# A transformer block on one core: a 1152x1152 matrix-vector section moved from TensorE to VectorE, with its weights loaded transposed and the loads around it reordered

## The chip, the core and the metric

The kernel runs on one core of a Trainium2 chip. The metric is device time in microseconds (us) of one execution. Most executions of one kernel agree within 0.3%. A profile is one execution recorded by the hardware profiler; its "span" is mostly some 1.8 us shorter than the device time of the same run, because the start and the end of the program are not in it. Engines: PE is TensorE (PEld its weight loads), DVE is VectorE, ACT is ScalarE, POOL is GpSimd, and SP is SyncE, which here does nothing but issue transfers.

## The reference

One block of a diffusion transformer: two batches (B = 2) of N = 256 tokens, width D = 1152 (9 times 128), two heads, MLP width 4608, bf16.

```python
mod = (_silu(c) @ w_mod).reshape(B, 6, 1, D)
shift_a, scale_a, gate_a, shift_m, scale_m, gate_m = [mod[:, i] for i in range(6)]
h = _layernorm(x, axis=-1) * (1 + scale_a) + shift_a
q, k, v = ...                       # h @ wqkv
attn = _softmax(jnp.einsum('bqhd,bkhd->bhqk', q, k) * Dh ** (-0.5), axis=-1)
a = jnp.einsum('bhqk,bkhd->bqhd', attn, v).reshape(B, N, D) @ wo
x = x + gate_a * a
h2 = _layernorm(x, axis=-1) * (1 + scale_m) + shift_m
m = _gelu(h2 @ w_fc1) @ w_fc2
return x + gate_m * m
```

Each of the six modulation sections is a product of two rows (`s = silu(c)`, one per batch) with a 1152x1152 slice of `w_mod`: 2.65 MB of weights for very little arithmetic. This case is about one of them, `scale_m`, which is not needed before the MLP.

## The kernel before

TensorE does the work in this order: K, Q, scores, V, attention times V of the first batch, output projection of the first batch, attention times V of the second batch, the two MLP sections `shift_m` and `scale_m`, output projection of the second batch, f1 (first MLP matrix), f2 (second). All weights come through one queue that SyncE feeds in program order. The parts that matter:

```python
# a section on TensorE: s is the stationary operand (32 columns wide), the weights are streamed: 36 matmuls
def vec_section(stat, w, name): ...
shift_m = vec_section(sT, w_shift_m, "shift_m")
scale_m = vec_section(sT, w_scale_m, "scale_m")
nc.vector.tensor_scalar_add(scale_m[:, :, 0:B], scale_m[:, :, 0:B], 1.0)
# ... used by the modulation of the second layer norm, in front of f1
```

```python
# a section on VectorE, as this kernel already does gate_m, late in the MLP where the engine is idle
def dot_section(wT, s_all, spill, dst):
    for j in range(KD):                       # KD = 9
        for b in range(B):
            nc.vector.scalar_tensor_tensor(
                spill, wT[:, j, :], 1.0, s_all[:, b, :], op0=ALU.mult, op1=ALU.mult,
                accum_out=dst[:, b * KD + j:b * KD + j + 1])
```

For this the weights must lie with the output column on the partition, so they are loaded by transposing transfers (`dma_start_transpose`), and the row `s` is broadcast to all partitions. The order of the loads on the queue, as the program gives it:

```python
w_q, w_v, w_gate_a, w_o, w_shift_m          # issued before the attention part
attn_transpose(0); attn_transpose(1)        # softmax results, transposed by a transfer SBUF to SBUF
w_scale_m, w_f1_0                           # behind the attention transposes
ln2_transpose(0) ... (3)                    # layer norm results, transposed the same way, into hT
w_f1_1 ... w_f1_3, s_all, w_gate_mT         # the last one by transposing transfers
```

Copies of the results of Q, V and attention times V out of PSUM alternate between VectorE and ScalarE (`evac`), and the first `MSPLIT = 8` row blocks of f1 are done one batch at a time, so that they can start before the second batch's modulation is finished.

## Time and profile before

The median is 245.28 us in three runs (245.0 to 245.95).

The timeline of TensorE in the stage that the change touches (start, length, line, what it did; a bracket would say how long the engine sat idle before it, and for what):

```profile
74.03 1.91 PE L530 MATMUL pa<-attnT_all,big 128*128 128x256 bf16 x16
75.87 0.63 PE L546 MATMUL pa<-attnT_all,big 128*64 128x256 bf16 x8
76.43 9.16 PE L612 MATMUL pacc<-w_o,big 128*128 128x384 bf16 x54
85.43 1.91 PE L530 MATMUL pa<-attnT_all,big 128*128 128x256 bf16 x16
...
88.38 1.28 PE L365 MATMUL pn<-w_scale_m,sT 128*32 128x288 bf16 x36
89.59 8.97 PE L612 MATMUL pacc<-w_o,big 128*128 128x384 bf16 x63
98.40 9.80 PE L707 MATMUL pacc<-hT,w_f 128*128 128x256 bf16 x82
```

No bracket: TensorE waits for nothing. The line of `w_scale_m` is what the change takes away; with the 36 matmuls of `w_shift_m`, left out here, it takes 2.32 us in the chain. And the timeline of SyncE, which shows when a transfer was handed to the queue and how long SyncE was held by it:

```profile
60.17 8.40 SPq L490 DMA_TRANSPOSE attnT_all<-soft  x2
...
127.86 15.03 SPq L685 DMA_TRANSPOSE w_gate_mT<-in_w_mod_dram  x3
```

The first transpose of attention is issued at 60.17; the records of its semaphore show it complete at 70.14, 3.9 us before TensorE needs it. The other line is for transposing loads of weights: three of 0.885 MB, of which the second and third took SyncE 4.02 and 4.13 us. A plain load of the same size takes 2.4 to 2.7 us.

### The profile page before, as it was taken

What the parts mean: (1) busy time and instruction counts of PE and PEld (TensorE: products, weight loads), DVE (VectorE), ACT (ScalarE), POOL (GpSimd) and SP (SyncE); (2) the same over time, 40 slices, a digit from 0 to 9 for tenths busy, and PEclk for the clock granted to TensorE, in tenths of its full rate; (3) what the DMA queues carried; (4) which work ended last, traced back from release to release, by engine and by line L of the source; (5) the groups of instructions that cost most, each with busy time, mean ns of one, the idle gap of its engine ahead of it and who ended that gap; (6) DMA issues with size and microseconds to landing.
All of it is one profiled execution on the core that took longest, in us unless ns stands there. A gap on an engine that the chain in (4) does not pass through costs nothing.

```text
span 243.1 us, 3903 instructions
## 1 busy us (share of the span) xinstructions
PE 237.1 (98%) x1652; PEld 139.4 (57%) x1652; DVE 83.7 (34%) x194; ACT 66.7 (27%) x130; POOL 31.3 (13%) x47
## 2 busy tenths in 40 slices
PE   8899999999999999999999999999999999999994
PEld 2585444465656676978444444444665666656674
DVE  3752462115635676720000019999002000000001
ACT  7632250133614075773322222333000000000000
POOL 1000013000310615200000000000314211111111
PEclk9999999999999999999999999999999999999999
DMA  6999999999999992299999999999891000000000
GB/s 231 328 334 362 370 327 313 363 362 336 374 235 347 342 193 49 49 236 330 326 327 273 246 206 337 327 326 280 240 282 49 16 19 16 16 20 27 22 16 19
DMA packets 70813, 53.89 MB, mean 222 GB/s; under 512 B 18939, under 2 KB 65419, under 8 KB 70795
## 3 DMA queue, kind: packets, MB, share of 16 engines
q1 hardware_dynamic: 70064, 52.43, 74.1%
q0 software_dynamic: 704, 1.20, 1.8%
q8 instruction: 13, 0.21, 0.4%
q14 instruction: 5, 0.04, 0.1%
q10 hardware_dynamic: 27, 0.00, 0.0%
HBM read 48.08 MB, written 1.19 MB: 203 GB/s over the span
## 4 chain that ended last, share of the span: by engine, by line
PE 93%; DMA 3%; DVE 1%; SPq 0%; ACT 0%; issue 0%; DVEq 0%
PE pacc L707 29%; PE pacc L767 29%; PE pacc L612 7%; PE pacc L503 7%; PE pacc L438 7%; PE pk L253 4%; DMA w_scale_a<-in_w_mod_dram 3%; PE pk L282 2%; PE pn L365 1%; PE pa L530 1%; PE ps_s L458 1%; PE pm L221 1%; DVE stats L163 1%; PE pt L231 1%; PE pg L398 0%; SPq L85 0%
## 5 line engine op out<-in xcount | busy, mean ns | idle before, releaser
L707 PE MATMUL pacc<-hT,w_f 128*128 128x512 bf16 (+1 forms) x396 | 71.0, 340 | 0.0
L767 PE MATMUL pacc<-w_f,gT 128*128 128x384 bf16 (+2 forms) x468 | 70.5, 314 | 0.0
L767 PEld LDWEIGHTS <-gT 128*128 128x128 bf16 x468 | 44.3, 98 | 26.3
L707 PEld LDWEIGHTS <-w_f 128*128 128x128 bf16 x396 | 38.7, 98 | 31.9 <-issue 0.7
L429 DVE SCALAR_TENSOR_TENSOR late<-w_gate_mT,late 128x1152 bf16<-128x1152 bf16 x18 | 24.4, 1357 | 38.0 <-DMA w_gate_mT<-in_w_mod_dram 37.4
L773 DVE TENSOR_TENSOR tmp<-pacc,gate 128x384 f32<-128x384 f32 (+2 forms) x13 | 6.8, 526 | 62.6 <-PE pacc L767 50.3
L744 ACT ACTIVATE gT<-pacc 128x512 bf16<-128x512 f32 x28 | 16.7, 597 | 37.7 <-PE pacc L707 37.7
L612 PE MATMUL pacc<-w_o,big 128*128 128x384 bf16 (+2 forms) x117 | 18.1, 314 | 0.0
L503 PE MATMUL pacc<-w_v,hT 128*128 128x384 bf16 x108 | 17.9, 326 | 0.0
L775 POOL TENSOR_TENSOR o_sb<-tmp,x 128x384 bf16<-128x384 f32 (+1 forms) x12 | 11.6, 972 | 47.6 <-DVE tmp L773 47.6
L438 PE MATMUL pacc<-hT,w_q 128*128 128x512 bf16 x81 | 17.7, 379 | 0.0
L612 PEld LDWEIGHTS <-big 128*128 128x128 bf16 x117 | 10.9, 98 | 7.1 <-DVE big L270 0.6
L503 PEld LDWEIGHTS <-hT 128*128 128x128 bf16 x108 | 10.4, 98 | 7.2 <-issue 0.5
L253 PE MATMUL pk<-big,w_k 128*128 128x256 bf16 (+2 forms) x90 | 13.4, 294 | 0.4 <-ACT big L240 0.4
L438 PEld LDWEIGHTS <-w_q 128*128 128x128 bf16 x81 | 7.8, 98 | 9.8 <-DMA w_q<-in_wqkv_dram 0.5
L618 POOL TENSOR_TENSOR x<-tmp,x_sb 128x384 f32<-128x384 f32 (+1 forms) x11 | 9.8, 888 | 17.4 <-DVE tmp L617 10.7
L420 POOL DMA_DIRECT2D gates_dram<-grow x4 | 2.0, 512 | 71.4 <-DVE grow L730 71.4
L253 PEld LDWEIGHTS <-w_k 128*128 128x128 bf16 x90 | 7.5, 97 | 3.4 <-DMA w_k<-in_wqkv_dram 0.3
L146 PE MATMUL pwarm<-zeros 128*128 128x512 bf16 x23 | 7.7, 483 | 1.2 <-DVE eps_t L92 1.2
L617 DVE TENSOR_TENSOR tmp<-pacc,gate 128x384 f32<-128x384 f32 (+2 forms) x13 | 6.7, 525 | 5.4 <-PE pacc L612 5.3
L595 ACT ACTIVATE hT<-hT,shift_m,scale_m 128x256 bf16<-128x256 bf16 x12 | 6.2, 588 | 3.8 <-DVE stats L624 3.3
L240 ACT ACTIVATE big<-pt,scale_a 128x256 bf16<-128x256 bf16 (+1 forms) x12 | 4.6, 434 | 9.3 <-PE pt L231 7.6
(96 smaller groups left out, 146.8 us busy)
## 6 DMA issues: line engine op xcount, KB each, us to landing
w_f<-in_w_fc_dram SPq DMA_DIRECT2D x14, 864.0 KB, 10.9
w_f<-in_w_fc_dram SPq DMA_DIRECT2D x2, 2592.0 KB, 11.8
w_f<-in_w_fc_dram SPq DMA_DIRECT2D x2, 1728.0 KB, 14.9
w_shift_a<-in_w_mod_dram SPq DMA_DIRECT2D x3, 864.0 KB, 11.3
w_q<-in_wqkv_dram SPq DMA_DIRECT2D x3, 864.0 KB, 12.0
w_v<-in_wqkv_dram SPq DMA_DIRECT2D x3, 864.0 KB, 10.5
w_gate_a<-in_w_mod_dram SPq DMA_DIRECT2D x3, 864.0 KB, 9.9
w_o<-in_wo_dram SPq DMA_DIRECT2D x3, 864.0 KB, 13.8
```

Source lines behind the costliest of these rows:

```text
L146: nc.tensor.matmul(dst[:], zeros[:, 0:P], zeros[:], start=True, stop=True)
L253: nc.tensor.matmul(pk[m][:, c0:c1], w_k[:, k, m * P:(m + 1) * P], hT0[:, k, c0:c1], start=(k == 0 and c0 == 0), stop=(k == KD - 1), skip_g ...
L429: nc.vector.scalar_tensor_tensor(spill, wT[:, j, :], 1.0, s_all[:, b, :], op0=ALU.mult, op1=ALU.mult, accum_out=dst[:, b * KD + j:b * KD + ...
L438: nc.tensor.matmul(pacc[:], w_q[:, k, m * P:(m + 1) * P], hT[:, k, :], start=(k == 0), stop=(k == KD - 1),)
L503: nc.tensor.matmul(pacc[:], hT[:, k, t * P:(t + 1) * P], w_v[:, k, pnl * PW:(pnl + 1) * PW], start=(k == 0), stop=(k == KD - 1),)
L612: nc.tensor.matmul(pacc[:], aT[:, k, t * P:(t + 1) * P], w_o[:, k, c0:c1], start=(k == 0), stop=(k == KD - 1),)
L618: (nc.vector if (t, i) in ((1, 2), (3, 3)) else nc.gpsimd).tensor_tensor(x1[:, t, c0:c1], tmp[:], x_sb[:, t, c0:c1], op=ALU.add)
L707: nc.tensor.matmul(dst, w_f1[m // KD][:, k, ml * P:(ml + 1) * P], hT[:, k, c0:c1], start=(k == 0), stop=(k == KD - 1),)
L744: nc.scalar.activation(gT[:, m, :], pacc[:], ACT.Gelu_apprx_tanh)
L767: nc.tensor.matmul(pacc[:], gT[:, kk, t * P:(t + 1) * P], w_f2[j][:, r, c0 - n * PW:c0 - n * PW + cw], start=(kk == 0), stop=(kk == KF - 1),)
L773: nc.vector.tensor_tensor(tmp[:], pacc[:], gate_m[:, b, c0:c0 + cw], op=ALU.mult)
L775: (nc.vector if last else nc.gpsimd).tensor_tensor(o_sb[:], tmp[:], x1[:, t, c0:c0 + cw], op=ALU.add)
```

## The change

The intent: take the 36 matmuls of `scale_m` (half of 2.32 us) off the engine that bounds the kernel, by giving them to VectorE, which is 34% busy, as 18 multiply-accumulate passes of 1.36 us. For that the section has to come transposed, and earlier, in slices between the loads of Q and V, and VectorE is relieved of the copies of Q and V. The core of the diff:

```diff
+    s_b = [work.tile([P, D], BF16, name="s_b", tag="xn", bufs=4) for _ in range(B)]
+    for b in range(B):
+        nc.sync.dma_start(s_b[b][:], s_dram[b:b + 1, :].partition_broadcast(P))
+    load_transposed(w_scale_mT, S_SCALE_M, 0)
+    load_panel(w_q, wqkv_v, 0, 2)
+    load_panel(w_v, wqkv_v, 2 * D, 0)
+    load_transposed(w_scale_mT, S_SCALE_M, CPP)
+    load_section("w_gate_a", S_GATE_A, w_gate_a)
+    load_panel(w_v, wqkv_v, 2 * D, 1)
+    load_panel(w_v, wqkv_v, 2 * D, 2)
+    load_transposed(w_scale_mT, S_SCALE_M, 2 * CPP)
+    w_o = load_panels("w_o", wo_v, 0)
...
+    scale_m_passes(0, KD)                      # nine passes ahead of Q's copies and softmax
     for m in range(KD):
...
-        evac(qT[:, m, :], pacc[:], attn_scale)
+        nc.scalar.mul(qT[:, m, :], pacc[:], attn_scale)
...
-        evac(v_sb[:, t, pnl * PW:(pnl + 1) * PW], pacc[:])
+        nc.scalar.copy(v_sb[:, t, pnl * PW:(pnl + 1) * PW], pacc[:])
...
-        if i == 1:
+        if i == 2:
+            scale_m_passes(KD, B * KD)         # nine passes behind the last softmax piece
+        if i == TPB + 1:
             gate_a = gate_natural(0, w_gate_a)
...
-    w_scale_m = load_section("w_scale_m", S_SCALE_M)
+    w_shift_m = load_section("w_shift_m", S_SHIFT_M)   # now behind the attention transposes
...
-    scale_m = vec_section(sT, w_scale_m, "scale_m")
-    nc.vector.tensor_scalar_add(scale_m[:, :, 0:B], scale_m[:, :, 0:B], 1.0)
...
-    MSPLIT = 8
+    MSPLIT = KD
```

(The two comments are added here. Left out: the rows `s` are written to DRAM earlier, so that they can be broadcast.) The product of `gate_a` also uses a wider stationary operand and one copy in place of four.

More of the change, by code (lines that the diff above doesn't have):

```diff
@@ L121, with load_panel, load_transposed @@
     w_shift_a = load_section("w_shift_a", S_SHIFT_A)
-    w_q = load_panels("w_q", wqkv_v, 0)
+    w_q = wide_tile("w_q")
+    w_scale_mT = wide_tile("w_scale_mT")
+    w_v = wide_tile("w_v")
     w_gate_a = wide_tile("w_gate_a")
-    w_v = load_panels("w_v", wqkv_v, 2 * D)
-    load_section("w_gate_a", S_GATE_A, w_gate_a)
-    w_o = load_panels("w_o", wo_v, 0)
-    w_shift_m = load_section("w_shift_m", S_SHIFT_M)
+    def load_panel(w, view, col0, n):
+        nc.sync.dma_start(w[:, :, n * PW:(n + 1) * PW], view[:, :, col0 + n * PW:col0 + (n + 1) * PW])
+    def load_transposed(w, s, j):
+        c0 = s * D + j * P
+        nc.sync.dma_start_transpose(w[:, j:j + CPP, :], w_mod[:, c0:c0 + PW])
+    load_panel(w_q, wqkv_v, 0, 0)
+    load_panel(w_q, wqkv_v, 0, 1)
     big1 = act.tile([P, 4 * KD, T], BF16, name="big1", tag="big")
@@ L285, in k_panel, with store_by_quadrant @@
             )
+    s_dram = tc.dram_tile([B, D], BF16, name="s_dram")
+    def store_by_quadrant(dst, src, rows):
+        for a in range(4):
+            nc.gpsimd.dma_start(dst[a], src[32 * a:32 * a + rows])
+    s_rows = work.tile([P, KD, SW], BF16, name="s_rows", tag="s_rows", bufs=1)
     CUT = 4 * P
@@ L299 @@
     norm1(0, 0, CUT, "d")
+    nc.vector.transpose(s_rows[:].rearrange("p k c -> p (k c)"), sT[:].rearrange("p k c -> p (k c)"))
+    store_by_quadrant(s_dram[:].rearrange("b (k a r) -> a b k r", a=4, r=32), s_rows, B)
     add0()
@@ L389, with scale_m_passes @@
     k_evac(8)
+    s_b = [work.tile([P, D], BF16, name="s_b", tag="xn", bufs=4) for _ in range(B)]
+    s_spill = work.tile([P, D], BF16, name="s_spill", tag="xn", bufs=4)
+    for b in range(B):
[9 more added lines that the diff above has]
+    w_o = load_panels("w_o", wo_v, 0)
+    scale_m = act.tile([P, KD, B], FP32, name="scale_m")
+    def scale_m_passes(p0, p1):
+        dot_passes(
+            w_scale_mT, [t[:] for t in s_b], s_spill[:], lambda j, b: scale_m[:, j, b:b + 1], range(p0, p1),
+        )
     gates_dram = tc.dram_tile([2, B, D], BF16, name="gates_dram")
@@ L398, in gate_natural @@
                 nc.tensor.matmul(
-                    pn[32 * i:32 * i + B, :], sT[:, k, 0:B], wg[:, k, i * CTW:(i + 1) * CTW],
+                    pn[32 * i:32 * i + SW, :], sT[:, k, :], wg[:, k, i * CTW:(i + 1) * CTW],
                     start=(k == 0), stop=(k == KD - 1), tile_position=(0, 32 * i),
@@ L402, in gate_natural @@
         nat = work.tile([P, CTW], BF16, name="nat", tag="nat", bufs=1)
+        nc.scalar.copy(nat[:], pn[:])
         for i in range(4):
             rows = slice(32 * i, 32 * i + B)
-            if i % 2 == 0:
-                nc.vector.tensor_copy(nat[rows, :], pn[rows, :])
-            else:
-                nc.scalar.copy(nat[rows, :], pn[rows, :])
             nc.gpsimd.dma_start(gates_dram[g, :, i * CTW:(i + 1) * CTW], nat[rows, :])
@@ L413, in gate_natural, with dot_passes @@
         return gate
-    s_dram = tc.dram_tile([B, D], BF16, name="s_dram")
-    def store_by_quadrant(dst, src, rows):
-        for a in range(4):
-            nc.gpsimd.dma_start(dst[a], src[32 * a:32 * a + rows])
-    s_rows = work.tile([P, KD, SW], BF16, name="s_rows", tag="s_rows", bufs=1)
-    nc.vector.transpose(s_rows[:].rearrange("p k c -> p (k c)"), sT[:].rearrange("p k c -> p (k c)"))
-    store_by_quadrant(s_dram[:].rearrange("b (k a r) -> a b k r", a=4, r=32), s_rows, B)
-    def dot_section(wT, s_all, spill, dst):
-        for j in range(KD):
-            for b in range(B):
-                nc.vector.scalar_tensor_tensor(
-                    spill, wT[:, j, :], 1.0, s_all[:, b, :], op0=ALU.mult, op1=ALU.mult,
-                    accum_out=dst[:, b * KD + j:b * KD + j + 1],
-                )
-    gate_a = None
+    def dot_passes(wT, s_b, spill, dst, passes):
+        for i in passes:
+            j, b = divmod(i, B)
+            nc.vector.scalar_tensor_tensor(
+                spill, wT[:, j, :], 1.0, s_b[b], op0=ALU.mult, op1=ALU.mult, accum_out=dst(j, b),
+            )
+    scale_m_passes(0, KD)
     for m in range(KD):
@@ L551, in pv_shared @@
         evac(aT[:, HC, :], pa[:].rearrange("p b q n -> p (b q n)"))
+    nc.vector.tensor_scalar_add(scale_m[:], scale_m[:], 1.0)
     pv_chunks(0, 0)
@@ L587, in ln2_transpose @@
         nc.sync.dma_start_transpose(hT[:, :, t * P:(t + 1) * P], xn2[t][:])
-    shift_m = scale_m = None
     def ln2_modulate(b, ks=range(KD)):
@@ L710, in f1_mm @@
         )
-    MSPLIT = 8
+    MSPLIT = KD
     for b in range(B):
         for m0 in range(0, MSPLIT, 2):
-            pacc = acc_tile([P, 2, N], "pacc")
-            for m in (m0, m0 + 1):
+            ms = range(m0, min(m0 + 2, MSPLIT))
+            pacc = acc_tile([P, len(ms), N], "pacc")
+            for m in ms:
                 for k in range(KD):
                     f1_mm(pacc[:, m - m0, :], m, k, b * N, (b + 1) * N)
-            if b == 0 and m0 == MSPLIT - 2:
+            if b == 0 and ms[-1] == MSPLIT - 1:
                 ln2_modulate(1)
-            nc.scalar.activation(gT[:, m0:m0 + 2, b * N:(b + 1) * N], pacc[:], ACT.Gelu_apprx_tanh)
+            nc.scalar.activation(gT[:, ms[0]:ms[-1] + 1, b * N:(b + 1) * N], pacc[:], ACT.Gelu_apprx_tanh)
     gcol = small.tile([P, SW], FP32, name="gcol", tag="gcol", bufs=1)
@@ L745 @@
         if m == 14:
-            dot_section(w_gate_mT, s_all, late[:, B, :], gcol)
+            dot_passes(
+                w_gate_mT, [s_all[:, b, :] for b in range(B)], late[:, B, :],
+                lambda j, b: gcol[:, b * KD + j:b * KD + j + 1], range(B * KD),
+            )
             gate_m = gate_m_finish()
```

## The prediction

> **What bounds the kernel now.** TensorE. The busy table gives PE 237.1 of 243.1 us (98%), and the chain of waits is 93% PE; from 33.5 us to the end it never leaves PE for more than 0.1 us. DMA is the hidden second limit: the slices show it full from 6 to about 85 us (300 to 390 GB/s), so loads there are only moved, not hidden.
>
> **What the change removes.** 36 matmuls on w_scale_m: the pair of section products takes 2.32 us in the chain (87.3 to 89.7), so half, 1.16 us, all critical. MSPLIT 9 instead of 8 keeps PE on the first batch's half about 1 us longer (8 steps take 7.86 us); the trace shows second-half matmuls spaced out at 106.4 to 107.7 while modulation (0.34 us a piece) catches up. Worth about 0.6 us. Together: -1.75 us.
>
> **What it adds.** 18 VectorE passes at 1.357 us plus 0.08 us of accumulator read, 1.40 us apart in the trace (the gate_m passes): 25.2 us. 12.6 us of them come before softmax, 12.6 us after it. Off the engine's total this is free (DVE is 34% busy); by position it is not:
> - First nine: the transposed chunk 0 lands at about 42 us, chunk 1 at about 52 us, so they end at about 56, where softmax's first maximum wants DVE at 55.05: 0.5 to 1 us late.
> - Last nine: program order puts them after the last softmax piece (ends 66.6 before; about 65 to 66 now without V copies on DVE). They end at 78 to 79. The attention-times-V copies that stay on DVE were taken from 74.7 before. The output projection then waits until about 78.7 for its third chunk, where PE arrives at about 76.8: about 2 us lost.
>
> **DMA.** w_scale_m's 2.65 MB move ahead of the attention transposes (shift_m moves behind them), as transposed loads. The gate_m ones are issued 4.0 to 4.1 us apart for 0.885 MB, that is about 217 GB/s, against 2.4 to 2.7 us for plain panels: some 4.5 us extra, plus 1.8 us for the two broadcast rows. The Trainium skill, "DMA: Bandwidth & Descriptors", section "Latency and other measured facts", gives 261 GB/s for transposed DMA; this trace is slower, and I use the trace. The same page ("Queues, rings and completion order") says a ring is consumed in order, so the attention transposes queue behind w_o. They landed at about 70.2 us before and were needed at 74; now I estimate 76.5 to 77.7, so PE waits about 3 us. This overlaps the DVE delay above, not adds to it. q panel 2 (needed 45.2, lands about 45) and v panel 1 (needed 62.4, lands about 62) are just in time; gate_a's broadcast lands at about 80, near its need.
>
> ScalarE takes all Q and V copies (0.60 and 0.48 us each); it fits.
>
> **Sum.** +3.3 us lost around 74 to 80 us, -1.75 us gained later: about 246.7 us. An 80% range: 244.1 to 249.3. Chances: faster by over 2% 0.01, within 2% 0.93, slower 0.06.
>
> **What would show it.** Right: the chain of waits leaves PE near 74 to 79 us, for the DMA of attnT_all or for DVE passes; waits of the attention-times-V or output-projection matmuls grow from under 0.6 to 2 to 4 us; span from there to the end shorter by about 1.7 us; the f1 matmuls run without gaps at the batch change. Wrong: attnT_all lands before 74 us, or DVE passes end before 75.
>
> **What would make it wrong.** Transposed loads of 384-column strips running near plain speed (then about 245.2, the DVE delay alone); a much later q panel 2 or chunk 1 delaying softmax (248 or more); softmax finishing earlier, so that even DVE is in time (about 243.6).

## More of the kernel before

The head of the page of the profile: the busy line, then from the 40 slices the rows of TensorE, of its granted clock (9 is 90% or more of full speed) and of the bytes that the transfers moved, then the chain of work that ended last.

```profile
span 243.1 us, 3903 instructions
...
PE 237.1 (98%) x1652; PEld 139.4 (57%) x1652; DVE 83.7 (34%) x194; ACT 66.7 (27%) x130; POOL 31.3 (13%) x47
...
PE   8899999999999999999999999999999999999994
...
PEclk9999999999999999999999999999999999999999
...
GB/s 231 328 334 362 370 327 313 363 362 336 374 235 347 342 193 49 49 236 330 326 327 273 246 206 337 327 326 280 240 282 49 16 19 16 16 20 27 22 16 19
...
PE 93%; DMA 3%; DVE 1%; SPq 0%; ACT 0%; issue 0%; DVEq 0%
```

TensorE is busy 98% of the span, at full clock throughout, and the chain is TensorE work nearly everywhere. The row of GB/s shows the second thing to know: up to slice 14 (about 85 us) the queue of transfers is full. A load that is added there does not fill a hole, it pushes everything behind it.

## The result, and the profile after

The changed kernel takes 251.59 us (median of six runs, 250.38 to 251.99), against 245.45 for the kernel before in the same rounds (six runs, 244.97 to 246.12). The ratio is 1.0242, with a 95% interval of 1.0213 to 1.0271: slower by over 2%. Ratios are the mean time of one kernel's fast runs over that of the other's of the same rounds, so they are not quite the ratio of the medians quoted. The outputs are right.

The same parts of the page as above:

```profile
span 249.3 us, 3878 instructions
...
PE 238.2 (96%) x1615; PEld 140.5 (56%) x1625; DVE 100.5 (40%) x216; ACT 71.8 (29%) x141; POOL 31.4 (13%) x47
...
PE   7899999999993999999999999999999999999994
...
PEclk9999999999997799999999999999999999999999
...
GB/s 236 325 323 362 365 262 266 263 336 349 214 323 348 385 326 126 25 100 320 329 326 332 214 222 276 328 329 327 199 317 102 32 16 18 16 17 18 16 31 16
...
PE 56%; ACT 2%; DMA 1%; issue 1%; DVE 0%; ACTq 0%; DVEq 0%
```

There is one hole, in the slice that holds 75 to 81 us, and beside it a dent in the clock. TensorE has 36 matmuls fewer and yet 1.1 us more busy time. The chain of work that ended last now leads from f1 back through the layer norm (ACT, a transfer) and is traced no further back than 96.14 us, so its shares cover only the time from there; it does not pass through the hole, which therefore has to be read from the waits and the timeline. Its timeline, beside the one above:

```profile
79.02 3.60 PE L556 MATMUL pa<-attnT_all,big 128*128 128x256 bf16 x16 [4.60 <-DMA attnT_all<-soft]
82.55 1.06 PE L572 MATMUL pa<-attnT_all,big 128*64 128x256 bf16 x8
83.54 9.31 PE L638 MATMUL pacc<-w_o,big 128*128 128x384 bf16 x54
92.69 1.91 PE L556 MATMUL pa<-attnT_all,big 128*128 128x256 bf16 x16
...
95.75 8.97 PE L638 MATMUL pacc<-w_o,big 128*128 128x384 bf16 x63
104.55 1.10 PE L731 MATMUL pacc<-hT,w_f 128*128 128x256 bf16 x8
105.88 2.34 PE L731 MATMUL pacc<-hT,w_f 128*128 128x256 bf16 x20 [0.22 <-ACT hT L621]
```

Subtract the start times of the same stages, and the whole 6.2 us of difference in span falls out, with its sign:

| what | us | from |
|---|---|---|
| everything up to the end of V | +0.39 | 79.02 - 4.60 against 74.03 (0.2 of it is there when Q starts) |
| wait for the transposed attention | +4.60 | the bracket |
| attention times V and the shared heads take 4.52 us, not 2.40 | +2.12 | 79.02 to 83.54, against 74.03 to 76.43 |
| first output projection | +0.15 | 83.54 to 92.69, against 76.43 to 85.43 |
| second batch's attention, then one section, not two | -1.10 | 92.69 to 95.75, against 85.43 to 89.59 |
| second output projection | -0.01 | 95.75 to 104.55, against 89.59 to 98.40 |
| f1 to the end | +0.05 | 144.75 against 144.7; the eight matmuls at 104.55 take 1.33 us for 0.87 us of work, so 0.46 us of gap is inside |

The second large term is not a wait. The windows view (busy time of each engine in a stretch, then the granted clock, the share of the transfer engines and GB/s) of the changed kernel:

```profile
76.00:78.00 2.00, 0.00 (x0) 0.00 (x0) 1.93 (x5) 0.00 (x0) 0.00 (x0) 0.87 1.21 368
78.00:80.00 2.00, 0.98 (x5) 0.73 (x6) 0.05 (x1) 0.00 (x0) 0.00 (x0) 0.50 1.10 316
...
84.00:86.00 2.00, 2.00 (x13) 1.13 (x11) 0.43 (x1) 1.58 (x2) 0.00 (x0) 0.92 1.04 387
```

The granted clock falls to one half at 77.49, some 3.1 us after TensorE fell idle, and is back at 84.31, so the matmuls that follow the wait run at half speed (one every 213 ns in place of one every 109). This is what the Trainium skill says on "TensorE: Matmul & The Clock Gate", Part 1, "What's actually happening": the clock drops to one half after an idle window of about 3.4 us and comes back after a busy one, and the window is free-running. This trace agrees, and so do the others: each spell of half clock inside a kernel is one or two times 3.41 us long (6.83 here, 3.41 in e1, e3, e8 and e12). Of the six runs of the changed kernel two have the mean clock of one such window (0.993), four that of two (0.984 to 0.986).

Why the transposed attention was late, in the timeline of SyncE:

```profile
31.92 6.77 SPq L132 DMA_TRANSPOSE w_scale_mT<-in_w_mod_dram  x1
...
40.00 8.84 SPq L132 DMA_TRANSPOSE w_scale_mT<-in_w_mod_dram  x1
...
55.91 9.41 SPq L132 DMA_TRANSPOSE w_scale_mT<-in_w_mod_dram  x1
65.42 4.04 SPq L118 DMA_DIRECT2D w_o<-in_wo_dram  x3
69.55 7.20 SPq L514 DMA_TRANSPOSE attnT_all<-soft  x2
```

Before, SyncE issued the first attention transpose at 60.17; now at 69.55, because it stands behind a transposing load that holds SyncE for 9.41 us and behind `w_o`. The semaphore records have it complete at 78.97 (70.14 before), and TensorE starts at 79.02.

VectorE, finally. This group line gives count, busy time and mean of the new passes, then the idle time before them with its releaser:

```profile
L454 DVE SCALAR_TENSOR_TENSOR s_spill<-w_scale_mT,s_b 128x1152 bf16<-128x1152 bf16 x18 | 24.4, 1358 | 7.8 <-DMA w_scale_mT<-in_w_mod_dram 7.3
```

The first nine end at 55.2, and softmax's first maximum is at 55.25, against 55.05 before: no delay. The last nine end at 77.84. VectorE was done before the transposed attention came.

So the first comparison leaves two theories for the 6.1 us:

- Theory A: the transposing loads, standing in the queue ahead of the attention transposes, cost much more queue time than assumed; the wait of 4.6 us and the halved clock that follows are consequences.
- Theory B (rival): VectorE is the real limit at that point. Its last nine passes end at 77.84, the copies that follow could not have started earlier, so even with timely transposes most of the loss would remain.

There are two smaller questions: what the halved clock alone costs, and where the expected gain of 1.75 us (1.16 for the matmuls, 0.6 for MSPLIT) has gone, as f1 to the end is no shorter.

### The profile page after: what moved, and what is told of

Same layout as the page of the kernel before. It is cut to its first block, busy times and chain, and to the rows that moved or that the text cites. A ratio compares the mean times of both kernels' runs of the same rounds, so it can differ in the third digit from the quotient of the medians.

```text
span 249.3 us, 3878 instructions
## 1 busy us (share of the span) xinstructions
PE 238.2 (96%) x1615; PEld 140.5 (56%) x1625; DVE 100.5 (40%) x216; ACT 71.8 (29%) x141; POOL 31.4 (13%) x47
## 4 chain that ended last, share of the span: by engine, by line
PE 56%; ACT 2%; DMA 1%; issue 1%; DVE 0%; ACTq 0%; DVEq 0%
PE pacc L795 28%; PE pacc L731 28%; ACT hT L621 2%; DMA hT<-xn 1%; ACT xn L604 0%; ACT rstd L595 0%; DVE tmp L801 0%; DVE o_sb L803 0%; ACTq L621 0%; DVEq L801 0%
## 5 line engine op out<-in xcount | busy, mean ns | idle before, releaser
L731 PEld LDWEIGHTS <-w_f 128*128 128x128 bf16 x405 | 39.6, 98 | 31.2 <-issue 0.8
L454 DVE SCALAR_TENSOR_TENSOR s_spill<-w_scale_mT,s_b 128x1152 bf16<-128x1152 bf16 x18 | 24.4, 1358 | 7.8 <-DMA w_scale_mT<-in_w_mod_dram 7.3
L769 ACT ACTIVATE gT<-pacc 128x512 bf16<-128x512 f32 x27 | 16.1, 597 | 36.5 <-PE pacc L731 36.5
L556 PE MATMUL pa<-attnT_all,big 128*128 128x256 bf16 x32 | 5.5, 346 | 4.6 <-DMA attnT_all<-soft 4.6
L444 POOL DMA_DIRECT2D gates_dram<-nat x4 | 2.1, 522 | 54.5 <-ACT nat L441 54.5
```

The source lines that it names most:

```text
L454: nc.vector.scalar_tensor_tensor(spill, wT[:, j, :], 1.0, s_b[b], op0=ALU.mult, op1=ALU.mult, accum_out=dst(j, b),)
L731: nc.tensor.matmul(dst, w_f1[m // KD][:, k, ml * P:(ml + 1) * P], hT[:, k, c0:c1], start=(k == 0), stop=(k == KD - 1),)
L769: nc.scalar.activation(gT[:, m, :], pacc[:], ACT.Gelu_apprx_tanh)
```

## The experiments

Fifteen runs were made, of thirteen kernels, in four groups, each group on one chip with its own runs of the kernel before. Times are medians; the ratio is against the kernel before of the same group.

| run | what it is | result right? | us | before | ratio, 95% |
|---|---|---|---|---|---|
| e1_attn_first | change, `w_o` behind the attention transposes | yes | 253.16 | 245.07 | 1.0328 (1.0291 to 1.0364) |
| e2_plain | change, plain loads for the transposing ones | no | 245.60 | 245.07 | 1.0029 (0.9999 to 1.0059) |
| e3_no_late | change without the last nine passes | no | 250.31 | 245.07 | 1.0221 (1.0191 to 1.025) |
| e4_filler | change, TensorE kept busy in the hole | yes | 250.20 | 245.07 | 1.0211 (1.0182 to 1.024) |
| e5_msplit | before, MSPLIT = 9 alone | yes | 245.72 | 244.98 | 1.0027 (1.001 to 1.0044) |
| e6_gate_strips | before, shape of the gate_m loads | yes | 245.41 | 244.98 | one look |
| e7_plain_pvact | e2 and attention-times-V copies on ScalarE | no | 245.01 | 244.98 | 0.9991 (0.9961 to 1.0021) |
| e8_rescue | change, with three repairs | yes | 248.46 | 244.98 | 1.0127 (1.0101 to 1.0153) |
| e9_drop_section | before without the 36 matmuls | no | 245.16 | 245.34 | 0.9984 (0.9956 to 1.0012) |
| e10_interleave | before, transposing and plain loads in turn | yes | 245.56 | 245.34 | one look |
| e11_msplit_look | e5 again | yes | 246.32 | 245.34 | one look |
| e12_after_msplit8 | change with MSPLIT = 8 | yes | 250.50 | 245.34 | 1.0208 (1.0191 to 1.0225) |
| e13_msplit_shift | e5, 32 more instructions on TensorE at the start | yes | 245.06 | 245.16 | 0.9998 (0.9977 to 1.0019) |
| e14_drop_shift | e9 again (the name misleads) | no, on purpose | 243.79 | 245.16 | one look |
| e15_drop_fine | e9, 32 more instructions on TensorE at the start | no | 244.12 | 245.16 | 0.9964 (0.9943 to 0.9985) |

### Is it the transposing of the loads? (e2_plain)

Everything of the change stays, order and bytes too, but the three loads come in untransposed, so `scale_m` is wrong (relative error 0.055).

```diff
-        nc.sync.dma_start_transpose(w[:, j:j + CPP, :], w_mod[:, c0:c0 + PW])
+        nc.sync.dma_start(w[:, j:j + CPP, :], wmod_v[:, j:j + CPP, s * D:(s + 1) * D])
```

> The changed kernel with the three transposed loads of w_scale_m replaced by plain loads of the same bytes (wrong result on purpose). Theory A, and that transposed loads cost 2.3 us each more than plain ones plus pauses around them: attention weights land 6 to 8 us earlier, before PE reaches them at 74.4; PE then waits about 2 us for DVE at the output projection; time about 246. If instead the bytes alone (order of the queue) were the cause, the transposes would still land after 76 us and the time stay above 249.

Measured: 245.60 us, ratio 1.0029. The timeline of TensorE:

```profile
74.16 1.91 PE L555 MATMUL pa<-attnT_all,big 128*128 128x256 bf16 x16
...
78.60 8.62 PE L637 MATMUL pacc<-w_o,big 128*128 128x384 bf16 x52 [1.54 <-DVE big L277]
```

No wait for the transposed attention and no half clock. It completes at 71.51, not 78.97: transposing alone costs 7.46 us at this point (what it consists of is taken up with e10), and the other 1.37 us of the delay (71.51 against 70.14) come from the two broadcast rows and the order. Theory A holds. Theory B is right in one small part: VectorE's passes do hold the projection, for 1.54 us. That is a wait too short to drop the clock.

The three loads complete at 40.74, 50.94 and 68.85 us in the changed kernel, and at 40.01, 47.54 and 62.06 here. The loss accumulates: 0.7, 3.4, 6.8 us. The windows view around the first of them, changed kernel and then this run:

```profile
36.00:38.00 2.00, 2.00 (x11) 0.90 (x10) 0.00 (x0) 0.66 (x2) 0.00 (x0) 1.00 0.60 113
38.00:40.00 2.00, 2.00 (x11) 0.88 (x9) 0.00 (x0) 0.66 (x2) 0.00 (x0) 1.00 1.28 290
```

```profile
36.00:38.00 2.00, 2.00 (x11) 0.90 (x10) 0.00 (x0) 0.65 (x2) 0.00 (x0) 1.00 1.04 382
38.00:40.00 2.00, 2.00 (x11) 0.94 (x10) 0.00 (x0) 0.66 (x2) 0.00 (x0) 1.00 1.09 340
```

The last column is the one to read: 113 and 290 GB/s, where the same bytes loaded plainly move at 382 and 340. Around a transposing load the queue is not slower throughout; it has stretches in which little moves.

### Is it VectorE? (e3_no_late, e7_plain_pvact)

e3 replaces the last nine passes by a memset (relative error 0.041).

```diff
         if i == 2:
-            scale_m_passes(KD, B * KD)
+            nc.vector.memset(scale_m[:], 0.0)
```

> The changed kernel without its second nine VectorE passes; all loads stay (wrong result on purpose). Theory A: the time stays at 251 to 252, since the attention weights land at 79 us all the same. Rival B (late passes hold PE): 246 to 249.

Measured: 250.31 us. TensorE waits 4.30 us for the transposed attention and the projection starts at 82.67, 0.9 us earlier than in the changed kernel; of this, 0.4 us is an earlier landing and the rest a shorter spell of half clock (attention times V 3.36 and 0.81 us, in place of 3.60 and 1.06), and both vary from run to run. It came out about 1 us lower than theory A had expected (though its ratio, 1.0221, and that of the change, 1.0242, lie within each other's intervals), but with no VectorE work at all in front of the copies 5 us of the loss remain: theory B falls as the main cause.

e7 takes the 1.54 us wait of e2 away, by giving the attention-times-V copies to ScalarE as well.

```diff
-            if b == 0:
-                evac(dst, src)
-            else:
-                nc.scalar.copy(dst, src)
+            nc.scalar.copy(dst, src)
```

> The second experiment (plain loads in place of transposed ones, wrong result on purpose) and besides all copies of attention-times-V on ScalarE. If the 1.5 us wait of PE for a VectorE copy is what the late passes still cost there, it goes and the time falls from 245.6 to about 244.2. If not, another wait takes its place and it stays at 245 to 246.

Measured: 245.01 us against 244.98, ratio 0.9991. The projection starts at 76.21 in one piece, the wait is gone, and f1 starts at 97.10 but has its gap until 98.50. Even with both known losses taken away, no gain shows in the time against the kernel before: the interval holds 1. The spans of the four runs (242.0 to 243.1, against 242.7 to 244.0 for the kernel before) would allow about half a microsecond. So something else eats part of the gain; see the part on f1 below.

### What does the half clock cost? (e4_filler)

Twenty dummy matmuls stand ahead of attention times V; they fill the hole that is there anyway, and the result stays right.

```diff
     nc.vector.tensor_scalar_add(scale_m[:], scale_m[:], 1.0)
+    warm(20, aux_tile([P, T], "pwarm3"))
     pv_chunks(0, 0)
```

> The changed kernel with 20 warm-up matmuls of 512 columns (about 4.3 us at full clock) on TensorE just before attention-times-V, to fill the wait for the attention weights (correct result). If the halved clock at 77.7 to 84.4 us follows from the 4.6 us of idle PE, the clock stays at full and about 1.9 us come back: 249.6. If the drop has another cause (power, the burst after the wait), it stays and the time stays at 251.5 or rises.

Measured: 250.20 us. The ratio, 1.0211 against 1.0242 for the change, does not separate the two (the intervals overlap); the trace does. The timeline of TensorE:

```profile
78.98 1.92 PE L556 MATMUL pa<-attnT_all,big 128*128 128x256 bf16 x16
...
81.39 9.11 PE L639 MATMUL pacc<-w_o,big 128*128 128x384 bf16 x54
...
104.83 3.44 PE L732 MATMUL pacc<-hT,w_f 128*128 128x256 bf16 x30 [0.22 <-ACT hT L622]
```

The clock stays at 1.00, attention times V starts at the same time as in the changed kernel, and the projection starts 2.15 us earlier (81.39 against 83.54). So the half clock does cost 2.1 us there. (That is a spell of two windows; in e3, with one, the same matmuls take 4.03 us in place of 2.40, so 1.6 us.) But f1 runs steadily only from 104.83, just 1.05 us earlier than 105.88: half was given back. The layer norm's transposes into `hT`, issued at 91.87 and 95.44, complete only at 99.15 and 99.95. Two things hold them. The `w_f1_0` panels went into the queue ahead of them, from 78.83 to 89.29, and the last is complete at 96.63. And an instruction fetch at 97.06 to 98.11 falls into them (a packet of 16,384 bytes on the instruction queue; what it does is shown with e10): the first comes 2.52 us after that panel, against 1.0 to 1.1 us in the changed kernel, e3 and e12, which have no fetch there. How much of the gain would have stayed without the fetch is not shown.

### Can the wait be moved away? (e1_attn_first, e8_rescue)

e1 puts `w_o` behind the attention transposes.

```diff
     load_transposed(w_scale_mT, S_SCALE_M, 2 * CPP)
-    w_o = load_panels("w_o", wo_v, 0)
...
+    w_o = load_panels("w_o", wo_v, 0)
     w_shift_m = load_section("w_shift_m", S_SHIFT_M)
```

> The changed kernel with one edit: the three loads of w_o are issued after the two attention transposes instead of before them (correct result). Theory A (the attention weights come late because their transposing DMA stands behind too much other traffic in the queue): they land about 8 us earlier, near 71 to 72 us, the 4.6 us wait of PE for them goes, so does the halved clock after it; what stays is a wait of about 2 us for DVE or for w_o; time about 246.5. Rival B (the late VectorE passes, which end at 77.9, hold PE through the copies of attention-times-V): hardly any gain, PE starts the output projection after 82 us, time 250 or more.

Measured: 253.16 us, the slowest of all, and 6.7 us above what I had expected. The wait for the transposed attention is gone (it completes at 70.01, TensorE arrives at 75.13), but then:

```profile
78.67 11.52 SPq L118 DMA_DIRECT2D w_f<-in_w_fc_dram  x3
90.30 7.28 SPq L614 DMA_TRANSPOSE hT<-xn  x2
```

```profile
101.61 0.27 PE L731 MATMUL pacc<-hT,w_f 128*128 128x256 bf16 x1 [1.55 <-ACT hT L621]
...
104.75 3.44 PE L731 MATMUL pacc<-hT,w_f 128*128 128x256 bf16 x13 [0.41 <-ACT hT L621]
```

SyncE is held by the f1 panels until 90.19, so the `hT` transposes are issued at 90.30 and complete at 100.05 and 100.86. TensorE waits 1.55 us at f1, then takes one matmul per modulated chunk, 0.49 us apart, and falls to half clock again from 104.59 to 108.01. With the attention transposes moved ahead, the layer norm's pay for the queue time of the transposing loads. Some 1.5 us of it is an instruction fetch at 97.97 to 99.01, as in e4: the first `hT` transpose comes 2.52 us after the last panel.

e8 combines three repairs: `w_o` behind the attention transposes, the attention-times-V copies on ScalarE, and the third panel of `w_f1_0` behind the second layer norm transpose.

```diff
-    w_f1[0] = load_panels("w_f1_0", wfc1_v, 0)
+    w_f1[0] = wide_tile("w_f1_0")
+    load_panel(w_f1[0], wfc1_v, 0, 0)
+    load_panel(w_f1[0], wfc1_v, 0, 1)
...
     ln2_transpose(1)
+    load_panel(w_f1[0], wfc1_v, 0, 2)
```

> The changed kernel with its own transposed loads, and three edits: w_o after the attention transposes, all copies of attention-times-V on ScalarE, and the third panel of the first f1 weights behind the second transpose of the normalized rows (correct result). If the damage is only the order in the queue, all waits go and it reaches 244 to 245. If the transposed loads take DMA time that the stage until f1 does not have, a wait for w_o, the transposed rows or the f1 panels takes their place: 246 to 249.

Measured: 248.46 us (247.77 to 250.16), ratio 1.0127. It is the best right version of the change, 3 us better than the change itself, and still 1.3% slower than the kernel before. The profile shows a wait of 0.92 us for `w_o`, whose panels complete at 74.55, 78.90 and 81.45, and a slow start of f1: `hT` completes at 95.81 and 98.42 (with an instruction fetch at 96.14 to 97.18), and from 99.23 to 103.26 TensorE takes single matmuls, 4.0 us for 0.9 us of work, and then has half clock from 103.64 to 107.05. But this profile is of the slowest of the six runs. It and one other (249.91) have a mean clock of 0.993; the four at 1.000 take 247.77 to 248.60, so the spell of half clock is not part of the median.

### Why did a transposing load cost more than in the model? (e6_gate_strips, e10_interleave)

The prediction had taken 4.0 to 4.1 us a load from the `gate_m` loads. Those differ in two ways: they have another shape (384 rows of 1152 columns; the new ones are 1152 rows of 384), and they stand back to back. e6 changes the shape in the kernel before.

```diff
     for r in range(0, KD, 3):
-        nc.sync.dma_start_transpose(
-            w_gate_mT[:, :, r * P:(r + 3) * P],
-            w_mod[r * P:(r + 3) * P, S_GATE_M * D:(S_GATE_M + 1) * D],
-        )
+        c0 = S_GATE_M * D + r * P
+        nc.sync.dma_start_transpose(w_gate_mT[:, r:r + 3, :], w_mod[:, c0:c0 + PW])
```

> The kernel before, with the three transposed loads of w_gate_mT cut as the change cuts w_scale_mT (1152 rows by 384 columns instead of 384 rows by 1152 columns), still back to back (correct result). If the shape made the change's transposed loads slow, the second and third issue take 6 us or more; if the neighbours did (each of the change's stands alone between plain loads and drains the queue at both ends), they take about 4.1 us, as before.

Measured: 245.41 us, issues of 6.74, 3.80 and 3.99 us. The shape is not the cause. e10 puts one plain panel of f1 behind each transposing load:

```diff
+        nc.sync.dma_start(w_f1[3][:, :, r * P:(r + 3) * P], wfc1_v[:, :, 3 * D + r * P:3 * D + (r + 3) * P])
```

> The kernel before with the three transposed loads of w_gate_mT each followed by one plain panel of the last f1 weights, instead of standing together behind all nine panels (correct result). One panel of 2.7 us is then behind the last transposed load, so the first VectorE pass, which needs all three, would start at about 142.4 us if neighbours cost nothing. If each switch between plain and transposed traffic costs about 1 us of idle queue, it starts at 144 to 146 us, and the transposed issues grow from 4 to 6 us or more.

Measured: 245.56 us in the one run, so no cost shows at that place, where nothing waits. The timeline of SyncE:

```profile
120.68 6.62 SPq L685 DMA_TRANSPOSE w_gate_mT<-in_w_mod_dram  x1
127.40 0.54 SPq L689 DMA_DIRECT2D w_f<-in_w_fc_dram  x1
127.98 6.73 SPq L685 DMA_TRANSPOSE w_gate_mT<-in_w_mod_dram  x1
...
135.40 6.10 SPq L685 DMA_TRANSPOSE w_gate_mT<-in_w_mod_dram  x1
```

One pair of a transposing load and a plain panel takes 7.30 and 7.42 us from issue to issue. Apart, they take 4.07 and 2.65, together 6.7. That looks like 0.6 to 0.7 us for standing alone among plain loads, but the two intervals are not clean. When the first load is issued, SyncE is held by what is still in the queue. And an instruction fetch falls into that load: one packet of 16,384 bytes on queue 8, the instruction queue of the profile's page, at 128.10 to 129.10 us. The core moves 290 GB/s just before it and 30 GB/s from 128.5 to 130.0. The semaphore records, which tell when a load is complete, are a better measure. By them the three plain panels come in at 133.83, 140.41 and 146.90, so a pair takes 6.58 and 6.49 us. Apart, by the same records, a transposing load takes 3.75 and 3.64 us (the kernel before) and a plain panel of f1 2.7, together 6.4. So transposing costs about 1 us over a plain panel, and taking turns 0.1 to 0.2 us more. The neighbours are not the cause either.

Such a fetch falls into the third transposing load of the changed kernel too, at 66.14 to 67.14 us. The windows view just before and just after it began:

```profile
64.50:66.00 1.50, 1.50 (x12) 0.91 (x10) 1.42 (x4) 1.50 (x6) 0.14 (x1) 1.00 1.27 290
66.50:68.00 1.50, 1.50 (x11) 0.92 (x10) 1.47 (x4) 0.48 (x1) 1.42 (x3) 1.00 1.46 35
```

The last column falls from 290 to 35 GB/s. The second transposing load is complete 3.02 us after the plain load in front of it, the third 4.43 us, 1.41 us more. All six profiles with these loads (the changed kernel, e1, e3, e4, e8, e12) have a fetch in the third, and there 4.43 to 4.50 us, against 3.01 to 3.03 for the second. A fetch that meets plain loads does not do this: around the one at 88.24 in the changed kernel the core moves 326 GB/s before and 320 after. No run moves the fetch in the changed kernel, so its cost is read from times that coincide, not shown by an experiment.

With it the 7.46 us of e2 can be placed, by when each load is complete, changed kernel against e2. The three transposing loads, each with the plain load right behind it, take 1.76, 2.09 and (without the fetch) 0.94 us more, together 4.8; the fetch 1.41; the panel of V in front of the second 0.84, for which no run shows a reason; the others together 0.4.

### Where did the gain at f1 go? (e5, e11, e12, e13)

e5 is the kernel before with MSPLIT = 9 alone.

```diff
-    MSPLIT = 8
+    MSPLIT = KD
```

(With it come the three lines of the change that allow an odd number of row blocks.)

> The kernel before with one part of the change alone: nine f1 steps split by batch instead of eight (correct result). The prediction said about 0.6 us, but in the changed kernel the trace shows ScalarE's part of the second batch's modulation held back by one more gelu (it starts 1.2 us after the data landed), and TensorE still has two short gaps. So 0 to 0.4 us: 244.7 to 245.1 against 245.1.

Measured: 245.72 us, ratio 1.0027 (1.001 to 1.0044): slower by 0.7 us where 0.6 us of gain was predicted. The waits view has one line for TensorE around 108 us, where the kernel before has none:

```profile
PE pacc L707 <- DVE hT L599: 0.8, 1, 0.8
```

TensorE waits for the modulation of the second batch, which starts at 107.96 in place of 106.03. Its transpose was issued at 102.88, 0.2 us later than before. A transfer counts its semaphore up in 16 parts. Of this one 15 had come at 106.31 and the last at 107.86. In the same stretch the trace has one packet of 16,384 bytes on queue 8, the instruction queue of the profile's page. The records do not name the transfer engine of a packet, so that the late part had to share its engine with this packet is inferred from the times:

```
packets of 16,384 bytes on the instruction queue near the hT transposes (us), read from the trace's records
before   90.6-91.6   110.2-111.3
e5       90.8-91.8   105.8-106.6    transpose issued 102.88, 15 parts at 106.31, last 107.86
e11      ...         106.2-107.2    transpose issued 103.1,  15 parts at 106.70, last 108.27
e13      91.0-91.9   102.2-103.1    transpose issued 103.87, all parts at 107.13
```

Plain loads show the same. In e13 (below) an f1 panel whose last part comes at 118.67 has it 0.12 us after the fifteenth; the next one, behind a fetch at 119.9 to 121.0, has it at 122.78, 1.42 us after the fifteenth.

The same kernel was looked at once more on another chip:

> The fifth experiment's kernel once more, for a second profile. There the second batch's transposed rows landed 5.0 us after issue instead of 3.3 to 4.1, and TensorE waited 0.76 us for them. If that belongs to the kernel, it shows again; if it was chance, the landing is back at 3.3 us, TensorE has no gap there, and the time is 244.5 to 245.0.

Measured: 246.32 us, a gap of 0.93 us at the same place, with the same picture. So the collision belongs to the kernel (its instruction stream reaches a fetch at that moment) and not to the one run.

If this is so, shifting the fetch must take the loss away. e13 does that without touching the MLP: the dummy matmuls that warm TensorE at the very start are cut into more, smaller ones, so that all later fetches fall elsewhere.

```diff
-    warm(18, pwarm)
+    for _ in range(50):
+        nc.tensor.matmul(pwarm[:, 0:P], zeros[:, 0:P], zeros[:, 0:P], start=True, stop=True)
```

> The fifth experiment's kernel (split of nine f1 steps alone) with its 18 warm-up matmuls of 512 columns at the start replaced by 50 of 128 columns: about the same time, but 32 matmuls more, so that the instruction fetch at 105.8 us comes some 3.5 us earlier (correct result). If the fetch on one DMA engine is what made the second batch's rows land 1.6 us late, they land at about 106.2, TensorE's 0.76 us gap goes, and the time is 244.3 to 244.7 against 245.2 before. If something else delays them, it stays at 245.7 to 246.

Measured: 245.06 us, ratio 0.9998 (0.9977 to 1.0019). The fetch is now at 102.2 to 103.1, the transpose lands whole at 107.13, and f1 has no gap:

```profile
99.60 12.63 PE L708 MATMUL pacc<-hT,w_f 128*128 128x256 bf16 x110
```

From the start of f1 to the end the profile has 144.5 us, against 144.7 for the kernel before and 145.4 for e5. So the loss of e5 goes with the collision, and MSPLIT = 9 without it is worth about 0.2 us in the profile and nothing that the timing can tell from zero. This shifts more than the fetch: in that profile half clock returns at the start, from 9.60 to 13.02 us, and TensorE starts Q 1.2 us later. Three of the six runs have this profile's mean clock (0.993) and take 245.29 to 245.84; the other three take 244.69 to 244.83, near the 244.3 to 244.7 that had been expected. So the finer warm-up has a cost of its own in half of the runs, and MSPLIT = 9 may be worth some 0.3 us; that is a choice of runs after the fact, and not shown. But the move of the fetch and the vanishing of the straggler came together. That the two share an engine remains an inference, though one that made the right forecast here.

e12 asks the same of the changed kernel, with MSPLIT back at 8.

```diff
-    MSPLIT = KD
+    MSPLIT = 8
```

> The changed kernel with this one part undone (eight split f1 steps, as before; correct result). The prediction said the split saves 0.6 us, so 252.2; the fifth experiment says it costs up to 0.7, so 250.9. I expect no clear difference from 251.6: 251.2 to 252.0.

Measured: 250.50 us. The time is inconclusive: f1 starts at 103.95, 0.6 us earlier than in the changed kernel (104.55), upstream of anything that MSPLIT touches, and it is another chip with another spell of half clock. The profiles say more: from the start of f1's steady part to the end they have the same 143.4 us (105.88 to 249.3 in the changed kernel, 105.46 to 248.9 here), so nine split steps save nothing there.

### What are the 36 matmuls worth? (e9, e14, e15)

The kernel before, load kept, but the section's matmuls dropped (`scale_m` = 1, relative error 0.041). This is the most that the change could have gained from them.

```diff
-    scale_m = vec_section(sT, w_scale_m, "scale_m")
-    nc.vector.tensor_scalar_add(scale_m[:, :, 0:B], scale_m[:, :, 0:B], 1.0)
+    scale_m = act.tile([P, KD, 32], FP32, name="scale_m")
+    nc.vector.memset(scale_m[:, :, 0:B], 1.0)
```

> The kernel before without its 36 matmuls for scale_m, their copy and the addition of one; the load stays and scale_m is a constant (wrong result on purpose). This is all that the change could gain there, without any of its costs. The prediction counted 1.16 us: 243.8 against 245.0. If the layer norm of the second row tile, which these matmuls covered, becomes the new wait at f1 (the changed kernel shows a 0.5 us gap there), only 0.5 to 0.8 us come out: 244.2 to 244.5.

Measured: 245.16 us, ratio 0.9984 (0.9956 to 1.0012): nothing, where 1.16 us were expected. The six runs spread more than usual (244.04 to 246.61). The profile is of the slowest: an instruction fetch at 94.4 to 95.4 meets the second layer norm transpose, of which 15 parts are complete at 94.85 and the last at 96.41, and f1 is steady only from 101.28. I took this for the same collision and expected it to repeat:

> The ninth experiment's kernel (36 matmuls removed, wrong result on purpose) once more for a second profile, beside the next one: the fetch near 94.4 us falls while the first batch's second transpose is in flight (91.6 to 96.5), and TensorE gets no steady start at f1 until 101.3 us.

It did not: 243.79 us, fetch at 93.1 to 94.0, transpose complete at 93.59 in all its parts, f1 steady from 98.46. The same kernel, on another chip, met no collision. For this kernel, then, it depends on the run, which would also explain the spread. The shifted version:

> The ninth experiment's kernel with the same finer warm-up, which moves the fetch at 94.4 us to about 89 us (wrong result on purpose). If the fetch took the gain of the removed matmuls, the transposed rows land at about 94.7 and the time is 244.0 to 244.4 and steady; if not, it stays near 245.2 with the wide scatter of the ninth experiment.

Measured: 244.12 us, ratio 0.9964 (0.9943 to 0.9985), so 0.9 us gained, with the fetch at 89.9 to 90.8 and no straggler. The timeline of TensorE:

```profile
96.83 1.12 PE L708 MATMUL pacc<-hT,w_f 128*128 128x256 bf16 x8
98.17 14.03 PE L708 MATMUL pacc<-hT,w_f 128*128 128x256 bf16 x123 [0.22 <-ACT hT L596]
```

There is the same small gap as in the changed kernel at 104.55 and 105.88: with 1.1 us of matmuls gone, TensorE arrives at f1 before the last modulated chunk of the first batch is ready. The second layer norm, not TensorE, sets the start of f1's steady part. The removal is therefore worth about 0.9 us when undisturbed; part of its 1.16 comes back in this gap. (Two of the six runs, 244.76 and 244.78, have the mean clock of 0.993 that e13 has with the same warm-up; the others take 243.46 to 244.18.)

## Why the prediction was wrong, point by point

The prediction was 246.7 us with a range up to 249.3; measured was 251.59.

1. **What bounds the kernel: right.** TensorE, with the queue of transfers as the hidden second limit up to 85 us. The change hit that second limit.
2. **The wait for the transposed attention: right in kind, wrong in size.** The prediction said that the attention transposes queue behind the transposing loads and `w_o`, and land at 76.5 to 77.7. They landed at 78.97, and TensorE waited 4.60 us, not about 3. The mis-sized term is "some 4.5 us extra" for the transposing loads; it measured 7.46 (e2). The other term, "1.8 us for the two broadcast rows", measured 1.37 with the order. Of the 7.46, the transposing loads and the plain loads right behind them make 4.8, close to the 4.5; what the sum has no term for is the instruction fetch that meets the third load, 1.41, and 1.2 us elsewhere. Without the fetch the transposes would have landed at about 77.6 (an estimate: 78.97 less 1.41), where the prediction had them, and TensorE would have waited some 3.2.
3. **The half clock: missing.** This is the step that fails outright: the sum's "+3.3 us lost around 74 to 80 us" takes a wait for its length alone. It measured 4.60 of wait and 2.12 of slow matmuls behind it. The prediction had an idle of about 3 us in its sum and counted it as 3 us. The idle of 4.6 us also dropped the clock, and the matmuls after it took 2.1 us more (e4 shows the 2.1 by taking only this away). The page of the Trainium skill that says so, "TensorE: Matmul & The Clock Gate", section "Why this matters for your kernels", asks for no idle gaps above about 3 us; the predicted wait lay right at it and this had to be in the range.
4. **VectorE's last passes: right.** Predicted to end at 78 to 79, they end at 77.84, and "this overlaps the DVE delay" is right: hidden behind the late transposes. Alone the delay would give about 245.2, said the prediction; e2, where only it remains, measured 245.60 with 1.54 us of wait.
5. **VectorE's first passes 0.5 to 1 us late for softmax: wrong, and harmless.** They end at 55.2, softmax starts at 55.25, 0.2 us later than before, which is also the offset that Q had already.
6. **The gain of 1.75 us: did not appear.** The matmuls' 1.16 show in the timeline (1.10), but 0.46 us of it came back as a gap at f1. Alone, undisturbed, they are worth 0.9 (e15). The 0.6 of MSPLIT was read from spaced-out matmuls; alone it was worth about 0.2 in the profile, and lost 0.7 through a collision with an instruction fetch (e5, e11, e13). Within the changed kernel the profiles show nothing from it (143.4 us of steady f1 and rest with nine steps and with eight, e12). The sign "span from there to the end shorter by about 1.7 us" did not come: from the start of attention times V to the end it is 170.3 us, 1.2 longer than the 169.1 before.
7. **"Wait shows in the chain of waits": wrong about the view.** The chain that ended last leads back from f1 to the layer norm and ends there. The hole has to be read from the waits and from the timeline.

In one sum: predicted +3.3 and -1.75; measured +0.4 (start), +4.6 (wait), +2.1 (clock), +0.2 (first projection), -1.1 (matmuls), and about 0 from f1 on, together +6.2.

What stays open: 1.2 us of the 7.46, a run of the changed kernel with its fetches moved, whether the late part and the fetched packet used the same transfer engine, and why the collision in e9 happens in some runs only. No right version that ran beats the kernel before: e13 and the kernel before are the same within the interval, and e8 is the best of the change.

## What to carry to other kernels

A change that takes a microsecond from the bounding engine and adds a slow kind of transfer to a full queue has to be costed at the queue first: look for the next small transfer behind it that somebody needs, and for its margin (3.9 us here), and for the instruction fetches: in the changed kernel one met a transposing load, which then came some 1.4 us later. A wait of TensorE of 4.1 to 4.6 us (the changed kernel, e3, e12) cost its length and the matmuls after it at half speed; one of 1.54 us (e2) cost its length alone; between them no run shows a case. And moving the wait by reordering one transfer helps only if the queue runs empty before the next one that is needed; here it stayed full until about 94 us, and the wait came back at f1.

## What the Trainium skill lacked or had wrong

- "DMA: Bandwidth & Descriptors", section "Latency and other measured facts", gives 261 GB/s for a transposing transfer with a non-contiguous middle dimension. Here, back to back, loads of 0.885 MB were complete 3.75 and 3.64 us after the one before (the kernel before), that is 236 and 243 GB/s; while one of them moves, the windows view shows 290 (the changed kernel, 64.5 to 66.0). No page that I read gives a cost for alternating transposing and plain transfers on one queue: 0.1 to 0.2 us per pair here (e10).
- "Runtime: NRT & Kernel Launch", section "Instruction fetch mechanics", calls the cost of crossing a 16 KiB block of instructions "one DMA tail-bump, mostly hidden". In these traces the fetches are packets of 16,384 bytes that take 0.9 to 1.8 us each, 12 or 13 in an execution. When one fell into a transposing load of weights, the core's transfers fell from 290 to 35 GB/s for 1.5 us (the changed kernel, 66.5 to 68.0; 30 GB/s in e10). When one fell into a small transfer that TensorE was waiting for, the transfer's last part came about 1.55 us after the other fifteen (e5: 106.31 and 107.86; e11: 106.70 and 108.27), and the kernel lost 0.7 us (e5). The page does not say what a fetch costs the transfers that it meets; that both used one transfer engine is inferred from the times.
- "TensorE: Matmul & The Clock Gate", Part 1, agrees with the trace in its window of about 3.4 us: the spells of half clock inside the kernels last 3.41 or 6.83 us. It says that for modelling the ramp may be neglected, as under 1% of a typical kernel; here one idle gap cost 2.1 us of 251.6, that is 0.8%, which was a third of the whole result.
